# Clustered attention and a routed expert layer: two heads' outputs in one product, GpSimd's subtractions in pieces, a multiplication on another engine, filler products

## The chip, the cores and the metric

The kernel runs on one NeuronCore of one Trainium2 chip. The metric is device time in microseconds: the median of three runs of the whole program.

## The reference

Sixteen heads (2 batches of 8) of 768 tokens and 64 columns attend within clusters: a query sees only the keys that have the same nearest centroid of 16. The result, 1536 tokens of 512 columns, goes through a layer of 8 experts, of which each token takes the best, up to a capacity of 384 tokens.

```python
q_assign = np.argmax(np.einsum('bhsd,hcd->bhsc', q_n, c_n), axis=-1)   # k likewise
mask = q_assign[:, :, :, None] == k_assign[:, :, None, :]
scores = np.where(mask, scale * np.matmul(q, k.transpose(0, 1, 3, 2)), -1000000000.0)
attn = np.exp(scores - np.max(scores, axis=-1, keepdims=True))
attn = attn / (np.sum(attn, axis=-1, keepdims=True) + 1e-09)
x = np.matmul(attn, v)                      # then (tokens, heads x 64)
logits = x @ w_gate                         # best of 8 experts, gate_w = its softmax
h = np.maximum(np.einsum('ecd,edf->ecf', disp, w1), 0.0)
y = np.einsum('ecf,efd->ecd', h, w2)
out[i] = gate_w[i] * y[expert_idx[i], pos[i]]
```

## The kernel before

The program has a prologue (centroids, the first clusters), an attention stage over 16 heads (some 300 us) and an expert stage. Numbers are kept as a rounded float plus its remainder, so that a product of full precision is made of three fast ones; the remainders are subtractions, on VectorE or GpSimd.

A head is 12 groups `g`: two halves of 384 queries by 6 tiles of 128 keys. A group makes the scores in `st_group` (L361, L362: the second product reads the row `Qs`, which holds the negative maxima), two exponentials on ScalarE (L370: `pf` and its rounded `ph`), the remainder `pl` for each two groups (`p_low`, L376: VectorE, or GpSimd for the groups in `POOL_PL`), and four groups later (`LAG`) the three products with the values (`pv_group`, L387). After six groups ScalarE writes half of the head's result `oT` (L391): 64 columns and, as row 64, the sums of the exponentials, by 768 queries. Beside it `max_tile` (L306, and the maximum on VectorE, L313) works on the next heads, and `max_rows` (L344 to L347) turns the maxima and sends them by DMA (`mr`) into the row `Qs`.

`out_stage` (L397) takes a finished head, in group 4 of the next (`G_OUT`): six fp32 products (L408), one for each 128 tokens, with a 65 x 73 matrix (identity, and the head's gate weights) turn `oT` and give the gate logits; VectorE then divides by the sums (L417, L418), scales the logits (L424), adds them to those of the earlier heads (L425) and scales the values into `x` (L426).

`hooks` hangs the remaining work on groups. Cluster scores for the pair of heads after next (`cl_scores`, L182) and their assignment (`cl_assign`: L220 to L233, one multiplication, L225, on GpSimd) stand in odd heads, the turn back (`cl_back`) and its DMAs of cluster rows `qkm` in even ones; `split` (L284, L293) and `split_v` (L170) make the remainders of q, k and v on GpSimd for later heads, with copies by SP's queue; `zero_fill` clears DRAM in heads 2 to 5; `gate(0)` decides the experts of batch 0 in head 8 and scatters its rows with six indirect DMAs on GpSimd (L527); `row0` (L588) reads the first rows back in head 9. Tiles that are turned, cluster scores, `gate` and `out_stage` share the one PSUM buffer `psT`.

Each engine runs its instructions in order; SP issues all plain loads and copies in order and stands when one of them has to wait. The order is recorded by hand in the prologue, and elsewhere chosen by a scheduler within stretches that barriers bound; from head 8 on there is none until the expert stage. `keep_warm` (L835) issues products on constants whose results nobody reads.

```python
nc.tensor.matmul(out=tp[:, t * OW:(t + 1) * OW], lhsT=oT[:, (t0 + t) * P:(t0 + t + 1) * P],
                 rhs=rhb[:, hh, :], start=True, stop=True)
```

## Time and profile before

| | us |
|---|---|
| median of three runs | 515.59 |
| the three runs | 516.54, 511.2, 515.59 |
| the profiled execution, its own time | 517.28 |
| its span | 515.5 |
| TensorE busy | 486.8 |
| VectorE busy | 374.7 |
| ScalarE busy | 318.2 |
| GpSimd busy | 148.1 |

Busy times of TensorE count each product with its modelled pipeline, so that products in a row overlap; how close they can follow is read from their starts. PE is TensorE, DVE VectorE, ACT ScalarE, POOL GpSimd, SP the engine that issues plain DMAs. A row of a timeline gives start, length, engine, line, operation, and in brackets the idle time before it with what ended it. Names after an operation are the tiles written and read.

### The profile page before, as it was taken

How to read it: one execution, taken by the hardware profiler on the slowest of the kernel's cores; microseconds unless marked ns; L12 is line 12 of the kernel's file. 1: busy time of each engine (PE TensorE's matmuls, PEld its weight loads, DVE VectorE, ACT ScalarE, POOL GpSimd, SP SyncE). 2: the span in 40 equal slices, each digit the busy share in tenths (PEclk: the TensorE clock that was granted, in tenths of full speed). 3: DMA queues.
4: the chain of work that ended last, by engine and by line, in shares of the span. 5: the costliest groups of instructions: out<-in, count | busy, mean ns of one | idle time of the engine just before them, and what ended most of it. 6: DMA issues, size and time to landing. Idle time of an engine off the chain costs nothing. (4 is left out here: it accounts for less than half of the span.)

```text
span 515.5 us, 8317 instructions
## 1 busy us (share of the span) xinstructions
PE 486.8 (94%) x2917; PEld 420.4 (82%) x2917; DVE 374.7 (73%) x650; ACT 318.2 (62%) x642; POOL 148.1 (29%) x122
## 2 busy tenths in 40 slices
PE   8789999989999997899999999999999999999994
PEld 7667988879889886788888866889898989898873
DVE  5796597987997889999988675584757565665411
ACT  3665497687786986878787853464645445373310
POOL 5677144464434545435100040001000000101001
PEclk9888698999999999999999999999999999999999
DMA  7456436777242453431201038676758484855001
GB/s 227 90 135 186 156 81 242 274 238 237 93 116 69 93 197 89 103 89 33 71 2 42 1 125 314 222 252 203 242 205 287 171 294 149 286 170 197 0 9 41
DMA packets 31152, 77.69 MB, mean 151 GB/s; under 512 B 4710, under 2 KB 5056, under 8 KB 31106
## 3 DMA queue, kind: packets, MB, share of 16 engines
q1 hardware_dynamic: 26162, 60.94, 38.6%
q0 software_dynamic: 4944, 16.15, 8.3%
q8 instruction: 27, 0.44, 0.3%
q14 instruction: 19, 0.16, 0.1%
HBM read 50.07 MB, written 17.45 MB: 131 GB/s over the span
## 5 line engine op out<-in xcount | busy, mean ns | idle before, releaser
L370 ACT ACTIVATE pf<-s 128x384 f32<-128x384 f32 x192 | 94.7, 493 | 58.0 <-PE s L362 46.5
L313 DVE TENSOR_REDUCE mx<-m 128x1 f32<-128x384 f32 x192 | 101.6, 547 | 23.6 <-PE m L306 22.2
L376 DVE TENSOR_TENSOR pl<-pf,ph 128x768 fp32r<-128x768 f32 x88 | 100.2, 1138 | 10.7 <-ACT ph L370 8.3
L132 DVE TENSOR_TENSOR ws<-wraw,ws 128x1024 fp32r<-128x1024 f32 x64 | 78.7, 1248 | 26.5 <-ACT ws L126 26.3
L370 ACT ACTIVATE ph<-s 128x384 fp32r<-128x384 f32 x192 | 94.3, 491 | 0.0
L742 PE MATMUL g<-xh,ws 128*128 128x256 f32 x448 | 80.6, 282 | 0.1
L126 ACT ACTIVATE ws<-wraw 128x1024 fp32r<-128x1024 f32 x64 | 66.0, 1052 | 20.8 <-DMA wraw<-in_w_dram 19.6
L674 PE MATMUL g<-ws,hh 128*128 128x512 f32 x240 | 76.5, 400 | 1.6 <-PEq L831 0.7
L306 PE MATMUL m<-Y,W 112*128 112x384 f32 (+1 forms) x192 | 69.7, 370 | 6.9 <-DVE mx L313 6.3
L387 PE MATMUL o<-pl,vh 128*65 128x384 f32 x192 | 66.8, 348 | 5.2 <-DVE pl L376 4.6
L742 PEld LDWEIGHTS g<-xh,ws 128*128 128x128 f32 x448 | 69.6, 190 | 1.1 <-DVE hl L747 0.3
L527 POOL DMA_INDIRECT out_dram<-y,row x17 | 16.5, 972 | 187.3 <-DVE y L667 135.9
L361 PE MATMUL s<-W,Y 112*128 112x384 f32 (+1 forms) x192 | 69.8, 364 | 0.0
L362 PE MATMUL s<-Qs,Y 97*128 97x384 f32 (+1 forms) x192 | 66.3, 350 | 1.1 <-DMA Qs<-mr 1.0
L387 PE MATMUL o<-ph,vh 128*65 128x384 f32 x192 | 66.2, 345 | 0.0
L387 PE MATMUL o<-ph,vl 128*65 128x384 f32 x192 | 66.1, 344 | 0.0
L742 PE MATMUL g<-xl,ws 128*128 128x256 f32 x224 | 63.1, 282 | 0.0
L746 ACT ACTIVATE hh<-g 128x256 fp32r<-128x256 f32 x56 | 21.4, 385 | 60.6 <-PE g L742 58.7
L674 PEld LDWEIGHTS g<-ws,hh 128*128 128x128 f32 x240 | 43.5, 188 | 11.5 <-issue 1.9
L306 PEld LDWEIGHTS m<-Y,W 112*128 112x128 f32 (+1 forms) x192 | 37.9, 198 | 16.2 <-DVE mx L313 14.7
L674 PE MATMUL g<-ws,hl 128*128 128x512 f32 x120 | 47.3, 394 | 0.3 <-DVE hl L647 0.3
L284 POOL TENSOR_TENSOR ql<-qv,W 64x768 fp32r<-64x768 f32 x15 | 29.2, 1947 | 49.3 <-ACT W L282 32.8
(184 smaller groups left out, 779.6 us busy)
## 6 DMA issues: line engine op xcount, KB each, us to landing
wraw<-in_w_dram SPq DMA_DIRECT2D x64, 512.0 KB
row<-xd SPq DMA_DIRECT2D x25, 260.0 KB
xd<-z POOLq DMA_DIRECT2D x7, 780.0 KB, 5.1
v<-in_v_dram SPq DMA_DIRECT2D x8, 390.0 KB
qv<-in_qT_dram SPq DMA_DIRECT2D x8, 384.0 KB
...
```

The costliest lines, as they stand in the source:

```text
L126: nc.scalar.activation(out=w[:, 0], in_=raw[c], func=AF.Copy)
L132: nc.vector.tensor_tensor(out=w[:, 1], in0=t, in1=w[:, 0].bitcast(F32), op=ALU.subtract)
L284: eng.tensor_tensor(out=ql[h][a], in0=d["q"][a], in1=W[a].bitcast(F32), op=ALU.subtract)
L306: nc.tensor.matmul(out=m[:, 0:HALF], lhsT=W[0:KA[h % 2], t * P:(t + 1) * P], rhs=Y1[0:KA[h % 2], j * HALF:(j + 1) * HALF], start=True, sto ...
L313: nc.vector.tensor_reduce(out=mxt[h][:, j, t:t + 1], in_=m[:, 0:HALF], axis=AX.X, op=ALU.max)
L361: nc.tensor.matmul(out=s[:, 0:HALF], lhsT=Y1[0:ka, ks], rhs=W[0:ka, qs], start=True, stop=False)
L362: nc.tensor.matmul(out=s[:, 0:HALF], lhsT=Y0[0:kb, ks], rhs=Qs[0:kb, qs], start=False, stop=True)
L370: nc.scalar.activation(out=o[:, g % 2], in_=s[:, 0:HALF], func=AF.Exp, scale=1.0 / float(D) ** 0.5)
L376: eng.tensor_tensor(out=pl, in0=pf, in1=ph.bitcast(F32), op=ALU.subtract)
L387: nc.tensor.matmul(out=ot[h, j][0:VW, 0:HALF], lhsT=lhs, rhs=r, start=(kt == 0 and n == 0), stop=(kt == NT - 1 and n == 2))
L674: nc.tensor.matmul(out=ps[:, 0:DM], lhsT=h[:, f, ts], rhs=w[:, a, fs], start=(f == 0 and n == 0), stop=(f == KF - 1 and n == 2),)
L742: nc.tensor.matmul(out=ps[:, 0:w_], lhsT=w[:, a, fs], rhs=x[e][:, k, :], start=(n == 0), stop=(n == 3 * KD - 1))
```

## The change

Heads 0 to 13 are turned in pairs. `gather` sends each head's row of sums to a buffer in DRAM; after the odd head it moves that head's 64 rows below the even head's, into one tile of 128 rows, and reads the pair's sums back as a tile of 128 x 12. `out_pair` runs in groups 9 and 11 of the next even head, three tiles of 128 tokens each time: one product of 144 columns gives both heads' values and logits, and VectorE scales by the reciprocal sums. Logits are kept for each head and added once, after the last pair of a batch. Heads 14 and 15 keep `out_stage`. `gate(0)` moves from group 5 of head 8 to its group 11, its steps up to group 1 of head 9. GpSimd's subtractions of `split` are made in three pieces, those of `split_v` and its share of `p_low` in two. The multiplication in `cl_assign` is on VectorE for head 9. The tile of v has one buffer where it had two, and v of the second pair is loaded after the prologue. Six filler products are added in the prologue, and one ahead of the first maximum of each of the first head's groups 0 to 5.

```diff
+    G_PAIR = (9, 11)
...
-        nc.gpsimd.tensor_tensor(out=lo[:, :, :, 0:VW], in0=v, in1=hi[:, :, :, 0:VW].bitcast(F32), op=ALU.subtract)
+        for j in range(2):
+            nc.gpsimd.tensor_tensor(
+                out=lo[:, j, :, 0:VW], in0=v[:, j], in1=hi[:, j, :, 0:VW].bitcast(F32), op=ALU.subtract
+            )
...
+    def minus(eng, out, a, b):
+
+        n = out.shape[-1]
+        w = n if eng is nc.vector else -(-n // 3)
+        for c in range(0, n, w):
+            cc = slice(c, min(c + w, n))
+            eng.tensor_tensor(out=out[:, cc], in0=a[:, cc], in1=b[:, cc].bitcast(F32), op=ALU.subtract)
...
-            eng.tensor_tensor(out=ql[h][a], in0=d["q"][a], in1=W[a].bitcast(F32), op=ALU.subtract)
+            minus(eng, ql[h][a], d["q"][a], W[a])
...
-            nc.gpsimd.tensor_tensor(out=Y0[a], in0=d["k"][a], in1=Y1[a].bitcast(F32), op=ALU.subtract)
+            minus(nc.gpsimd, Y0[a], d["k"][a], Y1[a])
...
-            eng.tensor_tensor(out=pl, in0=pf, in1=ph.bitcast(F32), op=ALU.subtract)
+            if eng is nc.vector:
+                eng.tensor_tensor(out=pl, in0=pf, in1=ph.bitcast(F32), op=ALU.subtract)
+            else:
+                for j in range(2):
+                    eng.tensor_tensor(out=pl[:, j], in0=pf[:, j], in1=ph[:, j].bitcast(F32), op=ALU.subtract)
...
+            if j == 1 and h < NH - 2:
+                gather(h)
...
+    def gather(h):
+
+        p, j = divmod(h, 2)
+        nc.sync.dma_start(out=srow[h:h + 1, :], in_=oT_t[h][D:VW, :])
+        if j == 1:
+            nc.sync.dma_start(out=oT_t[h - 1][D:P, :], in_=oT_t[h][0:D, :])
+            sums[p] = work.tile([P, 2 * NT], F32, tag="sums", name="sums", bufs=2)
+            nc.sync.dma_start(out=sums[p], in_=srow[h - 1:h + 1, :].rearrange("j (t p) -> p (j t)", p=P))
...
+    def out_pair(p, t0, t1):
...
+        if t0 == 0:
+            r = sums[p]
+            nc.vector.tensor_scalar(out=r, in0=r, scalar1=1e-9, scalar2=None, op0=ALU.add)
+            nc.vector.reciprocal(out=r, in_=r)
+        tp = psT.tile([P, 512], F32, tag="t", name="otp")
+        for t in range(n):
+            nc.tensor.matmul(
+                out=tp[:, t * RW:(t + 1) * RW],
+                lhsT=oT_t[2 * p][:, (t0 + t) * P:(t0 + t + 1) * P],
+                rhs=rhp[:, hp, :],
...
+        nc.vector.tensor_tensor(
+            out=xt[b, "h"][:, t0:t1, hs],
...
+        nc.vector.tensor_tensor(
+            out=xt[b][:, t0:t1, 2 * hp * D:2 * (hp + 1) * D].rearrange("p t (j d) -> p t j d", j=2),
...
+        if p == NP - 1 or p == 2 * NP - 2:
+            nh = 2 * hp + 2
+            nc.vector.tensor_reduce(
...
-        if i == H and g == 5:
+        if i >= 2 and i % 2 == 0 and g in G_PAIR:
+            t = G_PAIR.index(g) * TH
+            out_pair(i // 2 - 1, t, t + TH)
+        if (i, g) == (H, G_PAIR[1]):
             gens["g"] = gate(0)
-        if i == H and g >= 5:
-            next(gens["g"], None)
+        if (H, G_PAIR[1]) <= (i, g) <= (H + 1, 1):
+            for _ in range(1 + g % 2):
+                next(gens["g"], None)
...
-        if i >= 1 and g == G_OUT:
+        if i == NH - 1 and g == G_OUT:
             out_stage(i - 1)
...
-                    gens["c"] = cl_assign(pi, AS_MUL)
+                    gens["c"] = cl_assign(pi, nc.vector if i == H + 1 else AS_MUL)
...
         split(0, 2)
+        keep_warm(4, psM.tile([P, 512], F32, tag="m", name="warm"))
         cl_back0("k", tk)
+        keep_warm(2, psM.tile([P, 512], F32, tag="m", name="warm"))
...
                 if i == 0 and g < NT:
-                    max_tile(1, g, 0)
+                    max_tile(1, g, 0, warm=WARM1)
```

What the scheduler makes of it is shown at three places. The first is TensorE around the output products of the first pair, in head 2 (L387, now L410, are the products with the values; L361 and L362, now L376 and L377, the scores). Before, head 1's turn stands in group 4 of head 2:

```order
L306 MATMUL m<-Y_100,W_96 128x384
L387 MATMUL o<-ph,vh 65x384
L387 MATMUL o<-ph,vl 65x384
L387 MATMUL o<-pl,vh 65x384
L408 MATMUL otp<-rhb,oT 128x73 x6
L361 MATMUL s<-W_94,Y_98 128x384
L362 MATMUL s<-Qs_102,Y_106 128x384
```

Now, at the end of head 2, the pair's two halves of three products each:

```order
L321 MATMUL m<-Y_97,W_93 128x384
L410 MATMUL o<-ph,vh 65x384
L410 MATMUL o<-ph,vl 65x384
L410 MATMUL o<-pl,vh 65x384
L452 MATMUL otp<-rhc,oT 128x144 x6
L376 MATMUL s<-W_96,Y_100 128x384
L377 MATMUL s<-Qs_104,Y_108 128x384
L321 MATMUL m<-Y_97,W_93 128x384
L410 MATMUL o<-ph,vh 65x384
L410 MATMUL o<-ph,vl 65x384
```

and on VectorE, at the same place, the pair's sums (L448, L449) and its two halves (L462 logits, L468 values), with maxima and `pl` around them:

```order
L328 TENSOR_REDUCE mx<-m 128x1 x5
L392 TENSOR_TENSOR pl<-pf,ph 128x768
L328 TENSOR_REDUCE mx<-m 128x1
L448 TENSOR_SCALAR sums<-sums 128x12
L449 RECIPROCAL sums<-sums 128x12
L462 TENSOR_TENSOR lh<-otp,sums 128x3x16
L468 TENSOR_TENSOR x<-otp,sums 128x3x128
L462 TENSOR_TENSOR lh<-otp,sums 128x3x16
L468 TENSOR_TENSOR x<-otp,sums 128x3x128
L392 TENSOR_TENSOR pl<-pf,ph 128x768
```

The turn has moved from group 4 to behind group 11, and its six products stand in a row although each three need the buffer that VectorE reads; in head 6 it is the same, in head 4 one product stands between, and for the later pairs the halves are apart by four products or more.

The second place is SP's queue in heads 2 and 3, where head 1's result is done. `qkm` are the cluster rows, `mr` the maxima of head 3. Before:

```order
L266 DMA W_93<-qkm 16x768
L266 DMA Y_97<-qkm 16x768
L266 DMA W_95<-qkm 16x768
L266 DMA Y_99<-qkm 16x768
L279 DMA Y_107<-Y_99 32x768
L347 DMA Qs_104<-mr 1x6x128
L121 DMA wraw<-in_w_dram 128x1024 x4
L154 DMA qv<-in_qT_dram 128x768
```

and now, with the row of sums, the move of the odd head and the read of the sums:

```order
L273 DMA W_93<-qkm 16x768
L273 DMA Y_97<-qkm 16x768
L273 DMA W_95<-qkm 16x768
L273 DMA Y_99<-qkm 16x768
L428 DMA srow<-oT_694 1x768
L430 DMA oT<-oT_694 64x768
L362 DMA Qs_104<-mr 1x6x128
L432 DMA sums<-srow 128x12x1
L294 DMA Y_107<-Y_99 32x768
L125 DMA wraw<-in_w_dram 128x1024 x4
```

Three transfers have come in; the read of `sums` stands behind `mr` here and in head 4, and ahead of `mr` for later pairs.

The third place is GpSimd from the last subtractions ahead of the first gate: `ql` and `Y` are remainders of q and k, `vl` of v, `pl` of the exponentials. Before:

```order
L284 TENSOR_TENSOR ql<-qv,W_96 64x768
L293 TENSOR_TENSOR Y_108<-kv,Y_100 64x768
L170 TENSOR_TENSOR vl<-v,vh 128x12x65
L527 DMA xd<-x,gsi 3200x520 x6
L284 TENSOR_TENSOR ql<-qv,W_93 64x768
L293 TENSOR_TENSOR Y_105<-kv,Y_97 64x768
L225 TENSOR_TENSOR ceq<-ceq,c16b 128x384
L376 TENSOR_TENSOR pl<-pf,ph 128x768
```

and now:

```order
L284 TENSOR_TENSOR ql<-qv,W_96 64x256 x3
L284 TENSOR_TENSOR Y_108<-kv,Y_100 64x256 x3
L175 TENSOR_TENSOR vl<-v,vh 128x6x65 x2
L284 TENSOR_TENSOR ql<-qv,W_93 64x256 x3
L284 TENSOR_TENSOR Y_105<-kv,Y_97 64x256 x3
L395 TENSOR_TENSOR pl<-pf,ph 128x384 x2
L605 DMA xd<-x,gsi 3200x520 x6
L284 TENSOR_TENSOR ql<-qv,W_95 64x256 x3
L284 TENSOR_TENSOR Y_107<-kv,Y_99 64x256 x3
L175 TENSOR_TENSOR vl<-v,vh 128x6x65 x2
```

The six scatters have moved behind the two subtractions of head 12 and behind `pl` of head 9, and the multiplication `ceq` is no longer here.

## Rows read from the trace of the kernel before

**Rows 1.** The page's busy times by engine: us, share of the span, instructions.

```profile
PE 486.8 (94%) x2917; PEld 420.4 (82%) x2917; DVE 374.7 (73%) x650; ACT 318.2 (62%) x642; POOL 148.1 (29%) x122
```

**Rows 2.** Windows: length, busy us of each engine (instructions), clock, DMA share, GB/s.

```profile
200.00:220.00 20.00, 18.67 (x117) 16.02 (x116) 19.55 (x34) 16.01 (x36) 8.41 (x5) 1.00 0.27 67
```

**Rows 3.** Waits of PE between 49 and 300 us: total, times, longest.

```profile
PE m L306 <- DVE mx L313: 4.4, 9, 1.3
PE o L387 <- DVE pl L376: 3.0, 1, 3.0
```

**Rows 4.** Timeline of PE from 200 us: start, us, engine, line, operation, out<-in.

```profile
200.14 1.46 PE L408 MATMUL otp<-rhb,oT 65*128 65x73 f32 x12
201.40 0.42 PE L361 MATMUL s<-W,Y 128*128 128x384 f32 x1
201.66 0.34 PE L362 MATMUL s<-Qs,Y 128*128 128x384 f32 x1
```

**Rows 5.** Lines 838 and 408: durations ns min/median/max, first and last start.

```profile
L838 PE MATMUL mtd<-onef x12: 272/275/275, 19.7 to 20.9; 128*128 128x128 f32 x12
...
L408 PE MATMUL otp<-rhb,oT x192: 227/275/331, 62.2 to 298.8; 65*128 65x73 f32 x192
```

**Rows 6.** Groups by form on DVE: busy us, mean ns.

```profile
L425 DVE TENSOR_TENSOR lg<-lg,lt 128x48 f32<-128x48 f32 x13 | 9.6, 737 | 0.0
...
L426 DVE TENSOR_TENSOR x<-otp,r 128x384 f32<-128x384 f32 x15 | 8.2, 545 | 0.0
...
L418 DVE RECIPROCAL r<-r 128x6 f32<-128x6 f32 x15 | 2.8, 183 | 0.2
...
L424 DVE TENSOR_TENSOR lt<-otp,r 128x48 f32<-128x48 f32 x13 | 2.6, 200 | 0.2
...
L225 DVE TENSOR_TENSOR ceq<-ceq,c16b 128x384 bf16<-128x384 bf16 x1 | 0.3, 348 | 0.0
```

**Rows 7.** Timeline from 193 us, POOL, DVE and PE.

```profile
193.89 1.87 POOL L284 TENSOR_TENSOR ql<-qv,W 64x768 fp32r<-64x768 f32 x1
194.43 3.91 DVE L376 TENSOR_TENSOR pl<-pf,ph 128x768 fp32r<-128x768 f32 x1
195.68 1.83 POOL L293 TENSOR_TENSOR Y<-kv,Y 64x768 fp32r<-64x768 f32 x1
...
198.39 0.39 PE L387 MATMUL o<-pl,vh 128*65 128x384 f32 x1 [3.04 <-DVE pl L376]
```

**Rows 8.** Timeline from 69 us, POOL and DVE.

```profile
69.16 1.85 POOL L284 TENSOR_TENSOR ql<-qv,W 64x768 fp32r<-64x768 f32 x1 [2.41 <-PE s L361]
...
70.03 1.80 DVE L376 TENSOR_TENSOR pl<-pf,ph 128x768 fp32r<-128x768 f32 x1
...
70.97 2.56 POOL L293 TENSOR_TENSOR Y<-kv,Y 64x768 fp32r<-64x768 f32 x1
```

**Rows 9.** Timeline of ACT: second result of head 1, first of head 2.

```profile
74.85 0.50 ACT L391 ACTIVATE oT<-o 65x384 f32<-65x384 f32 x1
...
84.30 0.49 ACT L391 ACTIVATE oT<-o 65x384 f32<-65x384 f32 x1
```

**Rows 10.** Timeline from 101 us: SP's issue of `mr`, and PE waiting for it.

```profile
101.22 0.75 SPq L347 DMA_DIRECT2D Qs<-mr  x1
...
105.15 0.44 PE L362 MATMUL s<-Qs,Y 97*128 97x384 f32 x1 [0.97 <-DMA Qs<-mr]
```

**Rows 11.** The page's DMA queue of SP: packets, MB, share of 16 engines.

```profile
q1 hardware_dynamic: 26162, 60.94, 38.6%
```

**Rows 12.** Windows of 2 us, PE alone: busy us, clock, DMA share, GB/s.

```profile
42.00:44.00 2.00, 1.52 (x8) 1.00 0.49 101
...
46.00:48.00 2.00, 2.00 (x11) 0.63 0.90 311
...
58.00:60.00 2.00, 2.00 (x8) 0.50 0.00 0
60.00:62.00 2.00, 2.00 (x12) 0.96 0.00 0
```

More of the change, by code (lines that the diff above doesn't have):

```diff
@@ L79 @@
     ident = cs[:, C_ID:C_ID + P]
-    rhb = const.tile([VW, H, OW], F32, name="rhb")
+    RW = 2 * (D + E)
+    rhc = const.tile([P, NP * RW + 2 * OW], F32, name="rhc")
+    rhp = rhc[:, 0:NP * RW].rearrange("p (n o) -> p n o", n=NP)
+    rhb = rhc[0:VW, NP * RW:].rearrange("p (j o) -> p j o", j=2)
     cbr = const.tile([P, NP, 32], F32, name="cbr")
@@ L380, in pv_group @@
         if g == 0:
-            oT_t[h] = work.tile([VW, S], F32, tag="oT", name="oT")
+            if h % 2 == 0:
+                oT_t[h] = work.tile([P, S], F32, tag="oT", name="oT", bufs=2)
+            else:
+                oT_t[h] = work.tile([VW, S], F32, tag="oT1", name="oT1", bufs=1)
         if kt == 0:
@@ L391, in pv_group @@
             nc.scalar.activation(
-                out=oT_t[h][:, j * HALF:(j + 1) * HALF], in_=ot.pop((h, j))[0:VW, 0:HALF], func=AF.Copy
+                out=oT_t[h][0:VW, j * HALF:(j + 1) * HALF], in_=ot.pop((h, j))[0:VW, 0:HALF], func=AF.Copy
             )
+            if j == 1 and h < NH - 2:
+                gather(h)
     xt = {}
+    sums = {}
+    srow = dram.tile([NH, S], F32, name="srow")
+    def gather(h):
[5 more added lines that the diff above has]
+            nc.sync.dma_start(out=sums[p], in_=srow[h - 1:h + 1, :].rearrange("j (t p) -> p (j t)", p=P))
@@ new lines, in new_rows @@
+    def new_rows(b):
+        xt[b] = work.tile([P, NT, XR], F32, tag="x", name="x", bufs=2)
+        xt[b, "l"] = work.tile([P, NT, E], F32, tag="lg", name="lg", bufs=2)
+        xt[b, "h"] = work.tile([P, NT, H, E], F32, tag="lh", name="lh", bufs=1)
+        nc.gpsimd.tensor_copy(xt[b][:, :, DM + 1].bitcast(I32), cs[:, C_TOK + b * NT:C_TOK + (b + 1) * NT])
+        nc.gpsimd.memset(xt[b][:, :, DM + 2:XR], 0.0)
+    def out_pair(p, t0, t1):
+        b, hp = divmod(p, NP)
+        n = t1 - t0
+        if hp == 0 and t0 == 0:
+            new_rows(b)
+        if t0 == 0:
[8 more added lines that the diff above has]
+                rhs=rhp[:, hp, :],
+                start=True,
+                stop=True,
+            )
+        tv = tp[:, 0:n * RW].rearrange("p (t o) -> p t o", o=RW)
+        r = sums[p].rearrange("p (j t o) -> p t j o", j=2, o=1)[:, t0:t1]
+        hs = slice(2 * hp, 2 * hp + 2)
+        nc.vector.tensor_tensor(
+            out=xt[b, "h"][:, t0:t1, hs],
+            in0=tv[:, :, 2 * D:RW].rearrange("p t (j e) -> p t j e", j=2),
+            in1=r.to_broadcast([P, n, 2, E]),
+            op=ALU.mult,
+        )
+        nc.vector.tensor_tensor(
+            out=xt[b][:, t0:t1, 2 * hp * D:2 * (hp + 1) * D].rearrange("p t (j d) -> p t j d", j=2),
+            in0=tv[:, :, 0:2 * D].rearrange("p t (j d) -> p t j d", j=2),
+            in1=r.to_broadcast([P, n, 2, D]),
+            op=ALU.mult,
+        )
+        if p == NP - 1 or p == 2 * NP - 2:
+            nh = 2 * hp + 2
+            nc.vector.tensor_reduce(
+                out=xt[b, "l"][:, t0:t1],
+                in_=xt[b, "h"][:, t0:t1, 0:nh].rearrange("p t h e -> p t e h"),
+                axis=AX.X,
+                op=ALU.add,
+            )
@@ L399, in out_stage @@
         n = t1 - t0
-        if hh == 0 and t0 == 0:
-            xt[b] = work.tile([P, NT, XR], F32, tag="x", name="x", bufs=2)
-            xt[b, "l"] = work.tile([P, NT, E], F32, tag="lg", name="lg", bufs=2)
-            nc.gpsimd.tensor_copy(xt[b][:, :, DM + 1].bitcast(I32), cs[:, C_TOK + b * NT:C_TOK + (b + 1) * NT])
-            nc.gpsimd.memset(xt[b][:, :, DM + 2:XR], 0.0)
         oT = oT_t[h]
@@ L419, in out_stage @@
         lg = xt[b, "l"][:, t0:t1]
-        if hh == 0:
-            nc.vector.tensor_tensor(out=lg, in0=tv[:, :, VW:OW], in1=r.to_broadcast([P, n, E]), op=ALU.mult)
-        else:
-            lt = work.tile([P, NT, E], F32, tag="lt", name="lt")[:, 0:n]
-            nc.vector.tensor_tensor(out=lt, in0=tv[:, :, VW:OW], in1=r.to_broadcast([P, n, E]), op=ALU.mult)
-            nc.vector.tensor_tensor(out=lg, in0=lg, in1=lt, op=ALU.add)
+        lt = work.tile([P, NT, E], F32, tag="lt", name="lt", bufs=1)[:, 0:n]
+        nc.vector.tensor_tensor(out=lt, in0=tv[:, :, VW:OW], in1=r.to_broadcast([P, n, E]), op=ALU.mult)
+        nc.vector.tensor_tensor(out=lg, in0=lg, in1=lt, op=ALU.add)
         nc.vector.tensor_tensor(
@@ L949, in warm @@
         load_pair(2)
+        load_v(1)
         first_rows()
@@ L1012, in _prepare @@
     t["cb"] = cbm.reshape(P, H // 2, 32)
-    r = np.zeros((D + 1, H, D + 1 + E), wg.dtype)
-    r[:, :, :D + 1] = np.eye(D + 1, dtype=wg.dtype)[:, None, :]
-    r[:D, :, D + 1:] = wg.reshape(H, D, E).transpose(1, 0, 2)
+    RW, OW = 2 * (D + E), D + 1 + E
+    r = np.zeros((2 * D, H // 2 * RW + 2 * OW), wg.dtype)
+    rp = r[:, :H // 2 * RW].reshape(2, D, H // 2, RW)
+    rs = r[:D + 1, H // 2 * RW:].reshape(D + 1, 2, OW)
+    wh = wg.reshape(H, D, E)
+    for j in range(2):
+        rp[j, :, :, j * D:(j + 1) * D] = np.eye(D, dtype=wg.dtype)[:, None, :]
+        rp[j, :, :, 2 * D + j * E:2 * D + (j + 1) * E] = wh[j::2].transpose(1, 0, 2)
+        rs[:, j, :D + 1] = np.eye(D + 1, dtype=wg.dtype)
+        rs[:D, j, D + 1:] = wh[H - 2 + j]
     t["rh"] = r
```

11 lines of the change are left out of this document (5 added, 6 removed).

## The prediction

> **What bounds the kernel now.** I read the busy shares first: TensorE 486.8 us of the 515.5, VectorE 374.7 [rows 1]. An average hides the stages, so next the windows: in the middle heads TensorE has 18.67 of 20 us and VectorE 19.55 [rows 2]. Both are full there. TensorE's list of waits says which of the two is late: between 49 and 300 us TensorE stood 4.4 us for VectorE's maxima and 3.0 us for one `pl`, and for little else [rows 3]. So in the attention stage a microsecond taken off TensorE counts, unless VectorE is then late in its place; a microsecond off VectorE counts only where it ended one of those waits. The expert stage behind 300 us is not touched by the change, and I carry it over unchanged.
>
> I make the sum against the profiled execution's own 517.28 us (span 515.5 and 1.8 around it). That execution lies 1.7 above the median of the three runs, 515.59; they spread from 511.2 to 516.5.
>
> **Output products in pairs.** Before, one head's turn is 12 TensorE instructions (6 fp32 products in two passes) that start at 200.14; the next score product starts at 201.40 and its successor 0.26 later, where 0.17 is the rule; so a turn takes 1.35 us [rows 4]. After, seven pairs (heads 0 to 13) take 6 products of 144 columns each, and heads 14 and 15 keep the old form. What does 144 columns cost? A pass of 128 columns takes 275 ns, the shortest of 73 columns 227: 48 ns over 55 columns, 0.87 ns a column [rows 5]. The passes stream then for 0.87 x 144 = 125 ns, and 12 of 128 columns, between the starts 19.7 and 20.9, came 0.11 apart [rows 5]. I take 0.125 a pass: 12 passes 1.50 us a pair against 2 x 1.35 = 2.70. Saved: 7 x 1.20 = 8.4 us. Bounds: 0.11 (nothing extra for the wider product, 9.7 us saved), and 0.275, a pass not overlapped at all (3.3 a pair, 4.2 us lost).
>
> What it adds on TensorE: a pair is done in two halves of 3 token tiles, and both use the one `psT` buffer. In heads 2 and 6 the order has the two halves directly behind each other, in head 4 with a single product between. TensorE must then stand until VectorE has read the first half: 48 columns at about 0.20 and 384 at 0.55 [rows 6], and some 0.35 for the hand-overs (my estimate from the 0.17 and 0.18 of such small steps). That is 1.1 us, three times: +3.3. The other four pairs have other products between their halves and cost nothing. Bounds: 0 (the first half is read while the second waits for nothing) and 7 x 1.1 = 7.7.
>
> On VectorE two heads cost 2 x (about 0.18 for the sum + 0.18 + 0.20 + 0.74 + 0.55) = 3.7, one pair now 0.36 + 2 x 0.75 = 1.9. Most of the saving is `lg<-lg,lt`, 0.74 us on average for 48 columns, where its neighbour `lt` needs 0.20 [rows 6], which the change drops for heads 0 to 13. It also drops the wait behind it; I come to that now.
>
> **Pieces, and who holds VectorE up.** `pl` reads two SBUF tiles and so do GpSimd's subtractions. At 194.43 a `pl` took 3.91 us; GpSimd ran two subtractions back to back, to 197.51, and TensorE stood 3.04 for this `pl` [rows 7]. At 70.03 a `pl` began within a subtraction as well; it took only 1.80, and the second subtraction was the one that got longer, 2.56 for 1.83 [rows 8, 7]. So VectorE waits for what runs, and sometimes also for what is queued behind it. The Trainium skill (SBUF — State Buffer, "Who interferes with whom") has an exclusive lock for the whole instruction, whichever starts first; by that alone thirds of a subtraction would cut each wait to a third. The rows at 70.03 agree, the rows at 194.43 do not: VectorE lost its turn to a second instruction that had long been ready. Three pieces of one subtraction become ready together, like those two.
>
> So I give the pieces little. Without the clock (below) the waits of [rows 3] come to 7.4. The one of 3.04 goes, since the scatters now stand behind both subtractions and not ahead of them (the order of the change): -3.0. From the 4.4 behind maxima I take 2.0 for the dropped `lg` additions and 1.5 for the pieces: -3.5. Bounds for the two: 0 and -4.4. The pieces' own cost: 64 x 768 becomes three instructions; GpSimd is 29% busy over the span [rows 1], so a tenth of a microsecond more each is hidden, except for `pl` in pieces, for which a product may wait 0.1 to 0.2, eight times; I put 0 to 1.5 into the range.
>
> **Gate and one multiplication.** The multiplication moved to VectorE costs 0.35 there [rows 6] and no longer queues behind six scatters on GpSimd. The first gate goes from heads 8 to 9; its scatters land later, and SP's load of `row0` waits for them with the cluster rows of head 12 behind it. These are read some four groups later, so I cost it at nothing; if the cover is gone it is 1 to 3 us, once. `psT` is used by five steps in a row there; same cost, same range.
>
> **Sums through DRAM.** Each pair now sends two rows of sums to DRAM, moves 64 x 768 of the odd head, and reads 128 x 12 single numbers back. VectorE's first instruction of a pair waits for that read, and maxima and `pl` are queued behind it, for which TensorE waits. Time available: head 1's result is written at 74.85, and the products stand behind the next half's result, which was at 84.30 [rows 9]: some 9 us. Needed: 0.75 for an issue like that of `mr`, and 3.2 from its end until TensorE went on at 105.15 [rows 10], about 4 each way; two of them follow one another (write, then read): 8, and in heads 2 and 4 `mr` is issued between. What the 1536 four-byte pieces add is in no row. Lower bound 0, upper bound that each takes what an average packet took: 38.6% of 16 x 515.5 us over 26162 packets is 0.12 us [rows 11], 96 on each of 16 engines, 11.7 us. The nearest row is that of `mr`, equally small in bytes, so I take its 4 us for the read and a lateness of 0.2 in the mean: 7 x 0.2 = +1.4. The Trainium skill (DMA: Bandwidth & Descriptors, "Rules for kernel authors") says that a strided last dimension lowers to one descriptor per element and should be rearranged. No run shows it yet. By it the read would tend to the upper bound; that is the slower rival.
>
> **Fillers and the clock.** Between 42 and 44 us TensorE was busy for 1.52 of 2 us, at full clock. From 46 to 62 us the granted clock shows 0.63, then 0.50 in six windows, the last of them from 58 to 60, then 0.96 [rows 12]: 13.6 us at 1.2 GHz with TensorE busy throughout, 6.8 us lost. Six fillers now stand among the first head's maxima, six in the prologue. I give an even chance that this spell goes: -3.4. Their price: 24 passes at 0.11, 2.6 us, mostly where TensorE waits anyway; I count +0.9. Bounds of the whole: -6.8 and +2.6.
>
> **Sum.** -8.4 + 3.3 - 3.0 - 3.5 + 1.4 - 3.4 + 0.9 = -12.7; 517.28 - 12.7 = 504.6.
>
> **Rivals.** *The saved time comes back as waits.* VectorE is as full as TensorE [rows 2]; if all seven pairs stand 1.1 at the half (+4.4 over my sum) and the pieces and the dropped additions give nothing (+3.5), it is 504.6 + 7.9 = 512.5: no change. For it: 19.55 of 20 us. Against: VectorE loses 1.8 us a pair itself.
> *Sums come late (slower).* The read of single numbers takes the upper half of its bounds: 5 us beyond my value, on VectorE, seven times: 504.6 + 35 = 540. It turns slower than before from 1.8 us of further lateness a pair (12.7 / 7). For it: nothing else in the kernel reads single numbers, and two transfers in a row take 8 of the 9 us. Against: the order has VectorE reach this instruction late, behind six more maxima.
> *The clock is all of it.* No spell is left: 504.6 - 3.4 = 501.2; or it stays as it was: 508.0, and the rest of the change is worth 9.3.
>
> **How the numbers follow.** Forecast (498 to 510.4): 0.69, with both clock cases in it. Below that 0.06, all terms at their good ends. Waits give it back (510.4 to 520.7): 0.17. Late sums: 0.08. About 1%, 5.2 us, can be told from no change: faster 0.75, same 0.17, slower 0.08. The range holds the forecast, half of the good ends and the nearer half of the waits: 496 to 513.
>
> **What would show it.** Right: a pair's 12 passes take about 1.5 us; a gap near 1 us between the halves in heads 2, 4 and 6; no `pl` near 3.9 us; VectorE's first instruction of a pair without idle time on the read of sums. Wrong: `sums` as what ended VectorE's waits, more than 10 us in all; `pl` as long as before despite pieces (lock not shared by pieces); a spell at half clock before 62 us of the same length (fillers without effect); TensorE's waits for maxima above 4.4.

## The result, and the profile after

The changed kernel takes 517.6 us in the median of 20 executions (513.6 to 528.8), the kernel before 514.6 in 20 on the same chips; the ratio is 1.0074, 95% interval 1.0044 to 1.0103. Forecast were 504.6 and "faster". Medians below are over all executions; ratios leave out those over 1.5% above the fastest of the same kernel. The profiled execution: 520.92 us, span 519.1 (before 517.28 and 515.5).

Not the whole of it is late. The first result of head 4 (L414, before L391) is there at 107.70 us, before at 118.26: 10.6 us ahead. The next half ends at 126.56 (127.25). The first result of head 9 is again 4.9 us ahead, at 199.94 (204.87), that of head 10 is not, at 222.44 (222.35), and the last comes at 299.75 (297.54). So the gain came, and went twice: between 108 and 127 us, and between 200 and 222. After (timeline of ScalarE):

```profile
107.70 0.48 ACT L414 ACTIVATE oT<-o 65x384 f32<-65x384 f32 x1
...
222.44 0.49 ACT L414 ACTIVATE oT<-o 65x384 f32<-65x384 f32 x1 [0.41 <-PE o L410]
```

and before:

```profile
118.26 0.48 ACT L391 ACTIVATE oT<-o 65x384 f32<-65x384 f32 x1
...
222.35 0.46 ACT L391 ACTIVATE oT<-o 65x384 f32<-65x384 f32 x1
```

The lines that answer to [rows 1, 2, 3] and to `pl` and the pieces: the page's busy times, the window from 200 us, PE's waits from 49 to 300 us, and groups by line.

```profile
PE 481.7 (93%) x2857; PEld 412.6 (79%) x2857; DVE 365.1 (70%) x629; ACT 317.7 (61%) x642; POOL 166.8 (32%) x199
```

```profile
200.00:220.00 20.00, 14.73 (x74) 10.66 (x72) 13.40 (x23) 12.64 (x29) 13.97 (x13) 0.90 0.47 137
```

```profile
PE otp L452 <- DVE x L468: 4.8, 4, 2.2
PE m L321 <- DVE mx L328: 4.0, 3, 2.4
PE mtp L359 <- DVE mxx L334: 3.7, 5, 0.8
PE m L321 <- DMA Y<-qkm: 3.2, 1, 3.2
PE o L410 <- DVE pl L392: 1.1, 3, 0.5
PE s L377 <- DMA Qs<-mr: 0.8, 1, 0.8
PE o L410 <- issue: 0.4, 1, 0.4
```

```profile
L392 DVE TENSOR_TENSOR pl<-pf,ph 128x768 fp32r<-128x768 f32 x88 | 94.8, 1077 | 15.0 <-ACT ph L385 13.1 <-PE o L410 0.9 <-PE m L321 0.5
...
L284 POOL TENSOR_TENSOR ql<-qv,W 64x256 fp32r<-64x256 f32 x45 | 38.6, 883 | 42.8 <-issue 22.2 <-ACT W L297 17.4 <-ACT ph L385 3.0
...
L334 DVE TENSOR_TENSOR mxx<-mx 128x6 f32<-128x6 f32 x15 | 7.9, 524 | 0.2
```

TensorE is busy 5.1 us less over the span, as wanted, and its waits between 49 and 300 us have doubled, from some 9 us (7.4 in [rows 3], the rest in smaller ones) to 18. Where [rows 2] had 18.67 and 19.55 of 20 us, TensorE and VectorE now idle for a quarter and a third of the window. The mean `pl` has fallen from 1138 to 1077 ns, the mean `mxx` (the maxima of a head's two halves joined) has risen from 224 to 524.

**The first place** (timeline from 105 us, SP, DVE and PE). `mr` leaves SP at 105.81, the read of the second pair's sums behind it at 106.65; VectorE gets them at 111.16.

```profile
105.81 0.74 SPq L362 DMA_DIRECT2D Qs<-mr  x1
106.65 0.40 SPq L432 DMA_DIRECT2D sums<-srow  x1
...
109.37 0.90 PE L452 MATMUL otp<-rhc,oT 128*128 128x144 f32 x6
...
111.16 0.31 DVE L448 TENSOR_SCALAR sums<-sums 128x12 f32<-128x12 f32 x1 [1.38 <-DMA sums<-srow]
...
111.96 0.55 DVE L468 TENSOR_TENSOR x<-otp,sums 128x384 f32<-128x384 f32 x1
...
112.65 1.06 PE L452 MATMUL otp<-rhc,oT 128*128 128x144 f32 x6 [2.21 <-DVE x L468]
```

The second half needs the PSUM tile that VectorE still has to read, and VectorE waits for the sums: 2.21 us. Windows of 2 us behind it:

```profile
108.00:110.00 2.00, 2.00 (x15) 1.85 (x14) 1.78 (x3) 1.89 (x6) 0.00 (x0) 1.00 1.07 287
110.00:112.00 2.00, 0.44 (x4) 0.12 (x2) 0.70 (x4) 0.64 (x1) 1.27 (x2) 1.00 1.05 287
112.00:114.00 2.00, 1.35 (x8) 1.38 (x9) 0.75 (x4) 0.00 (x0) 1.35 (x3) 0.85 0.95 379
114.00:116.00 2.00, 2.00 (x10) 1.72 (x8) 1.76 (x3) 1.59 (x3) 0.00 (x0) 0.50 0.55 170
...
126.00:128.00 2.00, 2.00 (x10) 1.88 (x9) 1.54 (x3) 1.44 (x4) 0.00 (x0) 0.73 0.00 2
```

A "stand" is idle time of TensorE in front of a product. The granted clock falls to 1.2 GHz behind this one (0.50 in a window) and is back in the window from 126: some 6.8 us lost while TensorE is busy throughout. The 2.4 us stand at 98.6 to 101.0 had no such spell at half clock behind it, so a stand alone does not decide it.

**The second place** (timeline from 203 us, POOL, SP and PE).

```profile
203.96 0.56 SPq L294 DMA_DIRECT2D Y<-Y  x1
...
205.45 1.49 POOL L605 DMA_INDIRECT xd<-x,gsi  x1 [0.31 <-issue]
...
209.98 3.63 POOL L284 TENSOR_TENSOR ql<-qv,W 64x256 fp32r<-64x256 f32 x3 [3.04 <-ACT ph L385]
...
210.01 0.34 SPq L670 DMA_DIRECT2D row<-xd  x1
213.64 0.51 SPq L294 DMA_DIRECT2D W<-ql  x1
...
216.09 0.59 SPq L273 DMA_DIRECT2D Y<-qkm  x1
...
217.05 0.98 PE L321 MATMUL m<-Y,W 112*128 112x384 f32 x2 [3.25 <-DMA Y<-qkm]
```

The last scatter is issued by 206.9. Two engines then stand until 210.0: SP for the landing (`row0`), and GpSimd in front of `ql` of head 12. SP sends `ql` when its three pieces are done, and only then the cluster rows `qkm`. TensorE stands 3.25 us for these, until 217.05, and the clock is at half from 216 to 222:

```profile
216.00:218.00 2.00, 0.95 (x3) 0.88 (x4) 0.25 (x1) 0.00 (x0) 1.92 (x3) 0.50 0.38 75
218.00:220.00 2.00, 2.00 (x8) 1.60 (x7) 0.85 (x3) 0.49 (x1) 0.32 (x1) 0.50 0.70 148
220.00:222.00 2.00, 2.00 (x8) 1.65 (x7) 1.69 (x3) 1.47 (x4) 0.00 (x0) 0.50 0.34 3
222.00:224.00 2.00, 2.00 (x12) 1.84 (x11) 1.07 (x3) 1.40 (x4) 0.00 (x0) 0.84 0.49 99
```

From 217.05 on, where TensorE works again, that costs 2.8 us more. A stand of 1.38 us for a maximum, at 208.03, comes on top; what lies behind that one was not followed.

**Products and pieces** (timeline, PE at 183 us; POOL, DVE and PE at 131 us).

```profile
183.50 0.90 PE L452 MATMUL otp<-rhc,oT 128*128 128x144 f32 x6
184.13 0.43 PE L410 MATMUL o<-ph,vl 128*65 128x384 f32 x1
```

```profile
131.17 1.97 POOL L395 TENSOR_TENSOR pl<-pf,ph 128x384 fp32r<-128x384 f32 x2 [0.71 <-PE o L410]
131.20 0.99 DVE L334 TENSOR_TENSOR mxx<-mx 128x6 f32<-128x6 f32 x1
...
132.33 0.27 PE L359 MATMUL mtp<-cs,mxx 128*6 128x128 f32 x1 [0.79 <-DVE mxx L334]
```

A half takes 0.63 to the next product. `mxx`, 0.15 us where nothing disturbs it, takes 0.99 beside a piece of GpSimd's `pl`, and TensorE waits for it; such waits of 0.8 us stand at 55.8, 89.7, 132.3 and 165.4 us, and one of 0.4 at 239.2.

### The profile page after: what moved, and what is told of

It is laid out like the page before. It is cut to its first block, busy times and chain, and to the rows that moved or that the text cites. A ratio compares the mean times of both kernels' runs of the same rounds, so it can differ in the third digit from the quotient of the medians.

```text
span 519.1 us, 8321 instructions
## 1 busy us (share of the span) xinstructions
PE 481.7 (93%) x2857; PEld 412.6 (79%) x2857; DVE 365.1 (70%) x629; ACT 317.7 (61%) x642; POOL 166.8 (32%) x199
## 2 busy tenths in 40 slices
DMA packets 42671, 79.37 MB, mean 153 GB/s; under 512 B 15703, under 2 KB 16049, under 8 KB 42624
## 5 line engine op out<-in xcount | busy, mean ns | idle before, releaser
L392 DVE TENSOR_TENSOR pl<-pf,ph 128x768 fp32r<-128x768 f32 x88 | 94.8, 1077 | 15.0 <-ACT ph L385 13.1
L136 DVE TENSOR_TENSOR ws<-wraw,ws 128x1024 fp32r<-128x1024 f32 x64 | 77.3, 1227 | 27.2 <-ACT ws L130 27.1
L321 PE MATMUL m<-Y,W 112*128 112x384 f32 (+1 forms) x192 | 68.4, 365 | 7.9 <-DVE mx L328 4.2
L376 PE MATMUL s<-W,Y 112*128 112x384 f32 (+1 forms) x192 | 70.8, 369 | 1.5 <-ACT ph L385 1.3
L410 PE MATMUL o<-pl,vh 128*65 128x384 f32 x192 | 66.9, 348 | 3.6 <-DVE pl L392 1.9
L410 PE MATMUL o<-ph,vh 128*65 128x384 f32 x192 | 66.7, 347 | 0.0
L410 PE MATMUL o<-ph,vl 128*65 128x384 f32 x192 | 66.1, 344 | 0.0
L377 PE MATMUL s<-Qs,Y 97*128 97x384 f32 (+1 forms) x192 | 65.1, 347 | 1.1 <-DMA Qs<-mr 0.8
L284 POOL TENSOR_TENSOR ql<-qv,W 64x256 fp32r<-64x256 f32 x45 | 38.6, 883 | 42.8 <-issue 22.2
```

The costliest lines, as they stand in the source:

```text
L136: nc.vector.tensor_tensor(out=w[:, 1], in0=t, in1=w[:, 0].bitcast(F32), op=ALU.subtract)
L284: eng.tensor_tensor(out=out[:, cc], in0=a[:, cc], in1=b[:, cc].bitcast(F32), op=ALU.subtract)
L321: nc.tensor.matmul(out=m[:, 0:HALF], lhsT=W[0:KA[h % 2], t * P:(t + 1) * P], rhs=Y1[0:KA[h % 2], j * HALF:(j + 1) * HALF], start=True, sto ...
L376: nc.tensor.matmul(out=s[:, 0:HALF], lhsT=Y1[0:ka, ks], rhs=W[0:ka, qs], start=True, stop=False)
L377: nc.tensor.matmul(out=s[:, 0:HALF], lhsT=Y0[0:kb, ks], rhs=Qs[0:kb, qs], start=False, stop=True)
L392: eng.tensor_tensor(out=pl, in0=pf, in1=ph.bitcast(F32), op=ALU.subtract)
```

## The experiments

"Span times clock" is the span multiplied by its mean granted clock, in the mean over a kernel's executions: roughly the time at full clock. It is 503.3 us for the kernel before (102 executions beside the experiments, mean clock 0.982) and 505.8 for the changed one (0.977). It flatters a kernel with a low clock: among the 102 executions a hundredth of clock costs 4.3 us, and the product reckons 5.2, so of a difference between kernels that far apart about 1 us is not real.

**Where the scatters stand.** First `row0` alone, two heads later:

```diff
-        if (i, g) == (H + 1, 3):
+        if (i, g) == (H + 3, 3):
             row0.append(wra.tile([P, XR], F32, tag="z", name="row0", bufs=1))
```

> The changed kernel with the load of the first expert rows (row0) two heads later, so that SP does not stand for the scatters' landing (5.2 us at 204.5 to 210.0). Theory SP (that wait holds back the cluster rows of head 10): the 3.25 us stand before m at 217 us falls under 1 us and the time by 3 to 6 us. Theory GpSimd (the ql behind the scatters waits for their landing by itself, 3.04 us, and SP then stands for it at the send of ql): SP's 5.2 us go, the send of ql still leaves at about 213.6 us, a stand of over 2 us for qkm stays, the time moves by under 1.5 us.

Median 521.2 of 4, ratio 1.013 (0.993 to 1.033): too wide to tell a few microseconds. Its timeline decides: the theory of SP falls. SP no longer waits for the landing itself, but stands at the send of `ql` until 214.07, because GpSimd waits for the landing by itself, here with the landing named, and the rest follows as in the changed kernel:

```profile
211.01 3.04 POOL L284 TENSOR_TENSOR ql<-qv,W 64x256 fp32r<-64x256 f32 x3 [2.35 <-DMA xd<-x,gsi]
...
214.07 0.51 SPq L294 DMA_DIRECT2D W<-ql  x1
...
217.54 0.66 PE L321 MATMUL m<-Y,W 112*128 112x384 f32 x1 [4.42 <-DMA Y<-qkm]
```

Then the gate itself, to the end of head 9 (`row0` two heads later as well):

```diff
-        if (i, g) == (H, G_PAIR[1]):
+        if (i, g) == (H + 1, 8):
             gens["g"] = gate(0)
-        if (H, G_PAIR[1]) <= (i, g) <= (H + 1, 1):
+        if (H + 1, 8) <= (i, g) <= (H + 1, 11):
```

> The changed kernel with the gate of the first batch at groups 8 to 11 of head 9 instead of group 11 of head 8 to group 1 of head 9, and row0 two heads later: the scatters then stand behind both subtractions of head 12 and no subtraction behind them waits for their landing. If the scatters' landing is what holds head 9 and 10 up: no wait of GpSimd's ql of 3 us, no stand for qkm (3.25 us) and none of 1.4 us at 206.6, the half-clock spell at 216 to 222 us (3.3 us lost) stays out in most runs, the time falls by 4 to 8 us, to 509 to 513. Rival (half-clock spells come at one place or another anyway): the stands go, the mean clock stays at 0.974 to 0.985 and the time falls by 0 to 3 us.

Median 518.7 of 4, ratio 1.011 (0.996 to 1.025). Both old stands, 1.38 and 3.25 us, are gone, but a new one of 2.95 us for a maximum stands at 212.8: VectorE and ScalarE idle together from 208.7 to 212.2, beside the last scatters. The trace has only "remote" as what ended it, and I cannot explain it. So this run decides nothing. Clear of GpSimd's subtractions, in head 13 (`row0` in head 14):

```diff
+        if (i, g) == (13, 1):
             gens["g"] = gate(0)
+        if (13, 1) <= (i, g) <= (13, 4):
```

> The changed kernel with only the first batch's gate moved to head 13 (row0 to head 14); the pairs' halves stand where the change put them. If the scatters' place is worth by itself what latepairs won over the changed kernel: no wait for qkm, the heads 9 to 12 shorter by 5 to 7 us, span times clock at 498 to 501 us, median 506 to 510. If the halves are: the stands for x stay at 4 to 5 us, the gain is under 4 us, median 511 to 515.

Median 512.9 of 10, ratio 0.9975 (0.993 to 1.002), span times clock 502.0. No wait for `qkm`; TensorE's waits for `x` stay (5.6 us). The scatters' place cost the change about 4 us by span times clock. That brings it back to the kernel before; the forecast gain is still missing.

**Halves and sums.** A barrier between the halves:

```diff
+                if i in (2, 4, 6) and g == 10:
+                    tc.no_sync_barrier()
                 if len(todo) > LAG:
```

> The changed kernel with a scheduling barrier before group 10 of heads 2, 4 and 6, so that some ten TensorE rows stand between the two halves of a pair instead of none or one. If the halves' single PSUM tile costs what the trace shows (otp waits 1.07, 2.21 and 1.22 us, of which about 1.1 each is the tile): the wait for x falls from 4.8 us to under 2, heads 2 and 6 have none, head 4 keeps up to 1.2 for its sums, the time falls by 2 to 4 us, more where the half-clock spell behind head 4 (13.7 us in the profile) then stays out. Rival (the stand is covered: behind it wait exponentials and maxima that are late anyway): the wait moves to mx or pl, the time is the same within 1 us.

Median 521.5 of 10, ratio 1.008 (1.001 to 1.015): no gain. The stands in heads 2 and 6 shrink from 1.07 and 1.22 to 0.42 each, the one in head 4 stays at 1.80. With the gate in head 13 as well:

> The changed kernel with the gate in head 13 and only a barrier between the halves of heads 2, 4 and 6 (the products where the change put them, behind the sums by nothing). If the single PSUM tile was the loss of the halves: the waits for x fall to 2.5 to 3 us in all, span times clock 494 to 497 against 502 of gate13 and 492.7 of latepairs, median 504 to 508. If the late sums were (VectorE and the whole row behind it wait with the read of the sums): the wait in head 4 stays at 1.5 to 1.8 and so does a spell behind it, 499 to 502, median 510 to 513.

Median 513.9 of 10, ratio 0.9985 (0.9935 to 1.0036), no other than gate13's. Span times clock is 497.0, 5 us less than gate13's, but the mean clock is 0.972 against 0.982, and that takes it back: in its profile head 4 stands 2.0 us with 6.8 us lost to the clock behind it, and 8.5 us more are lost between 40 and 57 us. The same products without any wait for their sums (each pair scaled by the reciprocals of the pair before):

> The changed kernel in which each pair's products are multiplied by the reciprocals of the pair before (its own are formed after its second half), so no product waits for sums that are still on their way; the results are scaled by the wrong row sums. If the sums are late only in the second pair (TensorE stood 1.55 to 2.21 us there in five profiles, 1.07 to 1.24 us in the first and third pair): the stand between the halves in head 4 falls to 1.0 to 1.2 us like the others, the sums' price is 0.5 to 1.1 us in all. Rival (sums late in every pair, my forecast's rival of 540 us): the stands fall in heads 2 and 6 too, and the attention ends over 3 us earlier at the same clock.

One execution, 507.1 us: stands of 1.05, 0.69 and 0.85 us in heads 2, 4 and 6. In head 4 the changed kernel and its variants with the same order stand 1.55 to 2.21 us, so the late sums cost 0.9 to 1.5 us there; head 2 keeps its stand, head 6 loses 0.4 us of it, and the rival in which every pair is late falls. Now the halves behind the sums, in the odd head; the gate has to follow, to groups 2 to 5 of head 9, and `row0` to its group 7:

```diff
-        if i >= 2 and i % 2 == 0 and g in G_PAIR:
-            t = G_PAIR.index(g) * TH
-            out_pair(i // 2 - 1, t, t + TH)
+        if i >= 3 and i % 2 == 1 and g in (0, 2):
+            t = (g > 0) * TH
+            out_pair((i - 3) // 2, t, t + TH)
```

> The changed kernel with only the halves moved behind the sums (groups 0 and 2 of the odd head, 36 or more rows apart); the gate of the first batch, which needs the fourth pair, follows at groups 2 to 5 of head 9, so that its scatters stand in the same two heads as in the changed kernel. If the halves' stands (4.8 us) and the sums are the loss: no wait for x over 0.3, four pairs of heads 1.6 us shorter each, span times clock at 497 to 500, median 506 to 509. If the scatters are the loss: a stand of 3 to 4 us between 200 and 218 us stays, median 511 to 514.

Median 513.7 of 10, ratio 0.999 (0.994 to 1.003), span times clock 499.7, 6.1 less than the changed kernel's. No pair waits for `x` any more (0.3 us of cluster scores do), and the stretches of two heads from 66 and from 133 us take 31.8 and 31.5 us for 33.2 and 33.1. But SP's load of `row0` left only at 208.35, the move of the fourth pair's rows behind it at 208.75, and TensorE stood 4.0 us for that move at 213.65.

**Pieces and fillers.** The changed kernel with whole subtractions:

```diff
-        w = n if eng is nc.vector else -(-n // 3)
+        w = n
```

(and `vl`, `pl` whole likewise)

> The changed kernel with GpSimd's subtractions whole again (ql, Y0, vl and its share of pl), all else as changed. Theory A (the pieces give the gain away: three pieces of ql take 2.65 us where the whole took 1.95, and while pieces stand ready behind each other VectorE does not get its turn): the 3.3 us pl at 97 us and the 0.8 us stands before mtp (3.9 us in 6) go, TensorE's waits for mx and mxx fall from 8.1 us to under 5, the time falls by 3 to 5 us, to 511.5 to 513.5. Theory B (the gain is given away at two places, the late sums of the second pair and the scatters' landing, each followed by a spell at half clock): GpSimd's busy time falls by 10 us, TensorE's waits stay within 2 us, the time moves by under 1.5 us.

Median 518.8 of 4, ratio 1.012 (0.993 to 1.031); span times clock 505.4 against 505.8. The waits trade places (`pl` 4.3 for 1.1, `mtp` 2.1 for 3.7), so beside the pairs as they stand these four executions show no worth of the pieces; a gain of 1 or 2 us could hide in them. The reverse, the kernel before with the pieces alone, first one execution and then timed:

> The kernel before with GpSimd's subtractions in pieces and nothing else changed. By the forecast VectorE gets its turn between two pieces: pl over 1.5 us and the waits for mx (4.6 us) fall, the 3.04 us stand at 198 us shortens to 1.0 to 1.5. By the changed kernel's trace (pieces stand ready behind each other and VectorE gets no turn until the last one is done; three pieces cost 0.7 us more than the whole): some pl still take over 3 us, mtp waits 0.7 to 0.9 us behind pieces where it waited 0.4 once, the sum of TensorE's waits from 45 to 295 us stays at 9 us or rises, up to 12.

> The kernel before with the pieces alone, timed. If the single run stands (its wait for pl at the scatters 0.2 us instead of 3.0, for mx 2.7 instead of 4.6): span times clock 495 to 498, median 504 to 508 (its clock as before's, 0.981), faster by 1 to 2 percent. If it was a chance: 500 to 503 and median 510 to 513.

503.5 us in the single execution, then a median of 506.5 of 10, ratio 0.984 (0.9795 to 0.989), span times clock 497.3. Behind the scatters, where one `pl` took 3.91 us, none passes 1.02 (186 to 196 us), and PE's waits from 49 to 290 us are down to 5.5 us (before 8.8), most of it:

```profile
PE m L317 <- DVE mx L324: 1.5, 5, 0.7
PE m L317 <- issue: 1.5, 1, 1.5
PE s L373 <- DMA Qs<-mr: 1.4, 1, 1.4
PE mtp L355 <- DVE mxx L330: 0.4, 1, 0.4
```

The pieces alone bring 1.6%, and what I had expected by the changed kernel's trace, waits as long as before or longer, was wrong. The fillers alone, on the kernel before:

> The kernel before with the change's filler products alone (6 in the prologue, 6 beside the maxima of head 1). Theory 1 (the fillers keep the clock up early): the half-clock spell at 46 to 60 us goes in most executions, 3 to 7 us are gained, mean clock 0.985 to 0.99, 508 to 512 us. Theory 2 (a spell comes somewhere anyway, whatever the fillers do): mean clock 0.975 to 0.985 as before, time within 1.5 us of before's, the spells at other places. Span times clock then stays at 502 to 504 us in either case.

Median 511.0 of 10, ratio 0.995 (0.991 to 0.9985): span times clock 503.1 as before, mean clock 0.987 for 0.982. Theory 1, though 2.6 us fall short of its 3 to 7. Both together:

> The kernel before with the pieces and the fillers together, without pairs, without the moved gate. From the single runs (pieces alone: span times clock 496 us against 503; fillers alone: the same 503 at a clock of 0.988 instead of 0.982): span times clock 496 to 498, clock 0.985 to 0.99, median 502 to 507, faster than before by 1.5 to 2.5 percent. If the pieces' single run was a chance (their waits are short only when the draws of the lock fall so): waits for pl and mx back at 6 to 8 us, median 509 to 512. In the first case the pairs with the moved gate cost the changed kernel 10 to 14 us.

Four executions from 501.2 to 512.1, for which there is no interval; span times clock 497.1, as the pieces alone. In the profiled one 8.5 us were lost at half clock between 43 and 60 us in spite of the fillers. That is no exception: of the 16 profiled kernels with the fillers six lose 8.5 to 10.2 us between 38 and 62 us, more than the 6.8 of the kernel before [rows 12], and of the two profiles of the pieces without fillers neither loses more than 1.7 there. So bfill's ratio, half a percent, is all that speaks for the fillers.

**All waits out.** Halves as in late9, gate in head 13, `row0` in head 14:

> The changed kernel with its two stands taken out: the halves of a pair's product at groups 0 and 2 of the odd head behind it (some 36 rows apart, its sums over 1.2 us longer on their way) and the gate of the first batch in head 13, where GpSimd has no subtraction left, row0 in head 14. If the gain of the pairs was given back by these waits: no wait of otp for x over 0.3 us (4.8 before), none for qkm (3.25), none of 1.4 us at 206 us; 7 to 9 us less standing, 508 to 511 us at the same clock, faster than the kernel before by 0.5 to 1.5 percent. Rival (what was stood out there is stood out elsewhere: maxima and subtractions bound these heads as well): the waits move to mx, pl and mtp, the time falls by under 3 us, to 514 to 516.

Median 505.3 of 4, ratio 0.9815 (0.971 to 0.992), the lowest ratio of all, and below what I had expected (508 to 511); span times clock 492.7. PE's waits from 49 to 290 us:

```profile
PE m L321 <- DVE mx L328: 3.1, 4, 2.3
PE s L377 <- DMA sums<-srow: 2.8, 1, 2.8
PE ctp L189 <- PE o L410: 0.8, 2, 0.5
```

The 2.8 us are SP's queue once more (timeline from 263 us): the row load waited for the scatters, the seventh pair's sums behind it, and VectorE behind those.

```profile
263.91 0.35 SPq L670 DMA_DIRECT2D row<-xd  x1
...
266.45 0.37 SPq L432 DMA_DIRECT2D sums<-srow  x1
...
269.14 0.17 DVE L448 TENSOR_SCALAR sums<-sums 128x12 f32<-128x12 f32 x1 [4.83 <-DMA sums<-srow]
...
269.39 0.41 PE L377 MATMUL s<-Qs,Y 128*128 128x384 f32 x1 [2.80 <-DMA sums<-srow]
```

The same with whole subtractions:

> The latepairs kernel with GpSimd's subtractions whole again. If the pieces are worth as much beside the pairs as in the kernel before (6 us): waits for pl and mx rise by 4 to 7 us, median 509 to 513. If they are worth nothing beside the pairs (as the run of the changed kernel without pieces said, 502 to 508 us of span times clock against 502 to 510 with them): median 504 to 507, as latepairs.

Median 519.7 of 10, ratio 1.008 (1.004 to 1.013), span times clock 501.1: above both ranges that I had given, and beside late pairs the pieces are worth 2.7%. Then three ways to take the last wait out, by a barrier ahead of the load, by loading after the attention, and on GpSimd's queue:

```diff
-            nc.sync.dma_start(out=row0[0], in_=xd[0:P, :])
+            nc.gpsimd.dma_start(out=row0[0], in_=xd[0:P, :])
```

> The latepairs kernel with the load of row0 held back, by a scheduling barrier in head 14, behind the sums of the seventh pair on SP's queue (in latepairs it stood ahead of them and waited for the scatters' landing; VectorE then waited 4.8 us for the sums and TensorE stood 2.8 us at 266 us, with a half-clock spell behind it). If a wait on an in-order queue costs its stand and the spell behind it: that stand goes, heads 13 and 14 are 3 to 5 us shorter than latepairs' 29.1 us from the middle of head 13 to the last half, span times clock 488 to 491, median 499 to 504, faster than the kernel before by 2 to 3 percent. If the stand was covered by others: 491 to 494 and median 502 to 506.

> The latepairs kernel with row0 loaded at the start of the expert stage, so that the seventh pair's sums leave SP without waiting for the scatters' landing; no barrier, the attention's order otherwise as in latepairs. If the 2.8 us stand at 266 us and the spell behind it were a queue's wait: they go, the last two heads take 24 to 26 us instead of 29.1, median 498 to 502, faster than before by 2 to 3 percent. If the row load then comes late for the experts, up to 1.5 us of it come back as a wait for row at 285 us. If it was covered: 502 to 505 as latepairs.

> The latepairs kernel with the load of row0 issued on GpSimd's queue, behind the scatters that it waits for and with nothing behind it until the second gate, instead of on SP's queue ahead of the seventh pair's sums. If the queue's order was the cost: the last four halves of the attention take 23.9 us as in rows_last instead of 29.1, no wait for row over 1 us at the start of the experts, median 499 to 503, faster than the kernel before by 2 to 3 percent, its spread set by the half-clock spell at 37 to 60 us. If the stand comes back elsewhere a second time: 504 to 508.

Medians 504.8 of 6 (ratio 0.986, 0.981 to 0.991), 511.3 of 12 (0.993, 0.990 to 0.997) and 504.3 of 6 (0.985, 0.978 to 0.992). Span times clock is 498.6, 496.4 and 491.9. All three lose the stand: the last four halves take 23.9, 23.9 and 24.0 us for 29.1. The barrier moved other work (6.0 us of waits for maxima, for 3.1). Loading late gave it back at the start of the experts, and missed its range of 498 to 502:

```profile
294.01 1.11 PE L725 MATMUL rtp<-cs,row 128*128 128x128 f32 x4 [4.58 <-DMA row<-xd]
```

with 5.9 us at half clock behind it. On GpSimd's queue no wait came back, yet the time is latepairs' within its interval: its profiled execution lost 8.5 us to a spell from 39 to 57 us and 3.4 from 152 to 159, the second without a stand of over 0.5 us ahead of it.

## Why the prediction was wrong, step by step

The forecast was -12.7 us, the median moved by +3.0. The step that failed first is "Gate and one multiplication", put at nothing; the maxima and the clock failed too. That the sum started from the profiled execution, 2.7 us above the median before, makes the miss look smaller than it is.

**Products, -8.4: right, by two errors that cancel.** Fourteen turns of 1.26 us (62.22 to 63.48, with 1.25 to 1.29 for the others) against seven of 2 x 0.64: 17.6 - 9.0 = 8.7 us. I read 1.35 for the old turn, from one place, and put 1.50 for the pair, with a price per column taken from a median beside a minimum: the 73 columns have the same median of 275 ns [rows 5].

**Halves, +3.3: mechanism right, size near.** The stands are 1.07, 2.21, 1.22 and 0.28: 4.8 us. In prevsums, where no pair waits for its own sums, 2.6 are left; by that one execution the other 2.2 are the sums'.

**Sums, +1.4: near in size by luck, wrong in spread.** I spread a lateness of 0.2 over seven pairs; VectorE idled 2.1 us for them in two pairs, 1.38 and 0.70. The read took 111.16 - 107.05 = 4.1 us from the end of its issue in the one, 3.7 in the other, where `mr` took 3.2 [rows 10]: up to 0.9 more, and far from my upper bound of 11.7. The Trainium skill (DMA: Bandwidth & Descriptors, "Rules for kernel authors") says that a strided last dimension becomes one descriptor per element, and the trace agrees: packets under 512 B go from 4710 to 15703, and seven pairs have 7 x 1536 = 10752 numbers. The rival of 540 us fell all the same. What made the read late was where it stood: behind `mr` in head 4, and in latepairs behind `row0`.

**The `pl` stall, -3.0: gone, but not for the reason given.** I gave it to the scatters' new place. The pieces alone, with the scatters where they were, take it away, and the new place with whole subtractions has 4.3 us of waits for `pl` (whole). The new place brought its own stands instead, 1.38 and 3.25 us.

**Gate and `row0`, nothing: this step failed.** I named the wait of SP and "1 to 3 us, once" if the cover is gone. I did not look at what GpSimd does next: `ql` of head 12 waits for the landing whatever SP does (row0's run), and `qkm` is behind `ql` on SP. Taken away (gate13) it is 1.0074 to 0.9975, some 5 us with the clock.

**Maxima, -3.5: failed beside the pairs.** 4.4 became 4.0, and `mtp` went from 0.4 to 3.7: +2.9. In the kernel before, the pieces take the waits for maxima to 1.5 and 2.6 in two profiles. I gave the pieces 1.5 us in all; with the stall they bring 6 by span times clock. The Trainium skill's lock for the whole instruction (SBUF — State Buffer, "Who interferes with whom") would have given more than I did: by it waits shrink to a piece, and in pieces_alone the `pl` over 1.2 us lose 9.6 us in all beyond their 0.95 (before 15.4; all from 40 to 300 us). The rows have exceptions, a `pl` of 3.32 us at 97.13 in the changed kernel, over three pieces. And it does not hold in every order: beside late pairs these losses are 12.7 us in pieces and 12.3 whole, and in late9, with pieces, 15.7. Why the pieces give nothing in the changed kernel, 1.6% before and 2.7% beside late pairs, is only partly shown: behind 49 us `mxx` falls upon a piece in six heads of the changed kernel, with a wait of TensorE in five, while `mtp` waits once in pieces_alone and never for `mxx` in latepairs. The rest is open.

**Clock, -3.4 + 0.9: failed.** The spell of 46 to 60 us went, and others came: the windows of 20 us up to 300 lose 12.2 us before and 12.0 after. The fillers themselves did what I said, 2.6 us alone; in the changed kernel the spells behind the stands of the pairs and the gate undid it. The rival "the saved time comes back as waits" (512.5 us, chance 0.17) is what happened by its name, not by its mechanism: I had seven pairs standing for 1.1 each, where three stood for over 1 us, and no stand for the gate. The clock came on top, for which my sum had no line: a new stand was priced at its own length.

In waits, TensorE's sum from 49 us on was to fall by 1.8 (+3.3 - 3.0 - 3.5 + 1.4); it rose by some 9. That eats the 8.7 of the products. Of the 3.6 us by which the span grew, 2.2 are the attention's, of which these two numbers leave most unexplained, and 1.4 the experts', which I did not follow.
